# State decays of the first six attention units through DRAM on the GpSimd queue, instead of one-column matmuls and a copy

## Chip, cores and metric

One core of one Trainium2 chip runs the whole program. The metric is the device time of one execution in microseconds (us); three runs of the kernel before gave 713.31, 714.43 and 714.64 us, median 714.43.

## What is computed

Three layers follow each other. The first is an attention with a decaying state, for 4 batches and 8 heads of 48 columns over 768 positions:

```python
f = 1.0 / (1.0 + np.exp(-f_logit))
for t in range(S):
    state = f[:, :, t, :, None] * state + np.einsum('bhd,bhe->bhde', k[:, :, t], v[:, :, t])
    y[:, :, t] = np.einsum('bhd,bhde->bhe', q[:, :, t], state)
```

Its result, laid out as x of 3072 rows and 384 columns, goes through `h = x @ w_in; g = h - tanh(h); x = g @ w_out` with 2048 hidden columns. The third layer sends each row, if `x @ w_skip > 0`, to the best of 8 experts (`relu(x @ w1[e]) @ w2[e]`, weighted and added to x).

## The kernel before

The positions are cut into chunks of 128. A **unit** u is one chunk of one batch (batch u % 4), 24 in all; two units make a block of 256 rows for the second layer. Within a unit the decay is a running sum of logarithms: `pl` (PE) sums the logs of the 128 rows, `ek` and `en` (ACT) take exp of the sum and of its negative, and `mk` and `mq` (DVE) scale k and q by them. `tk`, `tq` (PE) and `ck`, `cq` (ACT) transpose both, `scores` (PE), `mask` (DVE) and `values` (PE) make the unit's output, `out1` and `out2` (ACT) copy it out, `tails` (small DMAs, by POOL for units 1 and 3 and half of unit 5, by ACT for the other half, by SP later) move 16 rows of each head pair to their place, and `xhi` (ACT) and `xlo` (DVE) split the block into a high and a low part for the products of the second layer. Only the odd unit of a block has `tails`, `xhi` and `xlo`.

Between units of one batch the state `S` must be renewed: `renew` (DVE) adds the unit's sum of k times v, and `decay` (POOL, which is GpSimd) multiplies S by the decay over the whole unit. That decay is the last row (position 127) of the tile that `en` wrote, 8 heads by 48 columns; it must come to lie down the partitions, as a tile `dd` of 112 partitions by 4, one such slice for each unit of a block. There are two ways:
- Units 0 to 5 (`u < FIRST`, FIRST is 6): at the end of `values` eight matmuls with one column each (L594) turn the row into columns of PSUM, and `renew` begins with a copy of them (L631) to `dd`.
- Units 6 to 23: `put_dec` (L505) stores the row to the DRAM tensor `dec`, and `get_dd` (L637) reads it back, for the two units of a block, by an access that puts 448 single words of 4 bytes into 112 partitions by 4. Both are issued by SP. `decay` and `in_range` (DVE, a check on the size of the decays) wait for `get_dd`.

The second layer runs in slots, one for each 128 hidden columns of a block: `G` (PE, L737, into `ph`), `T` (ACT, tanh, L743, into `th`), `bend` (DVE, L748), `ghi` (ACT, L756) and `glo` (POOL, L762), which split the result into `gs`, and `H` (PE, L779). `th` has two buffers, so `T` of slot n waits for `glo` of slot n - 2. The weights of the second layer come in 16 chunks that must be unpacked on ACT and DVE in the same stretch: `ldw` and `ld` (three indirect DMAs by POOL for a chunk pair of w_in, L367, into `stgw`; one DMA by SP for w_out), `abs`, `shift`, `stt1`, `stt2`, `hi`, `lo`.

Each engine takes its instructions strictly in the order in which they are written. That order is a list of steps, `OPENING`, written out by hand as a string up to slot 28 (in `in_order`, `listed`); the rest follows from a planner with costs. A name and a number stand for a step there: `glo.0` is `glo` of slot 0, `decay.3` is `decay` of unit 3, `ldw.4.0`, `ldw.4.1` and `ld.4` are the three loads of chunk pair 4, which is the second pair of w_in.

The tile that `en` writes (`en0`, `en1` and a part of `early`) is written again by a later unit; `read` names the step that must have read it by then. The tensor `dec` is filled with ones at the start (`preset`), so that its pad words are set.

Of the kernel before, what the change touches and what calls it, by code (L numbers as in the profile page):

```python
# [97 lines left out]
def decay_attention_moe_kernel(  # L98
# [14 lines left out]
    nc = tc.nc  # L113
# [340 lines left out]
    def attend(u):  # L454
# [4 lines left out]
        kp, qp = kpad[i], qpad[i]  # L459
        i, ze = (u, -1) if u < 3 else ((u - 3) % 2, u - 3 if u < 5 else u - 2)  # L460
        e8 = epad[i]
        read = ("values" if ze < FIRST else "put_dec", ze)
        kp8, qp8 = kp[:, :, :D], qp[:, :, :D]
        kp4 = kp.rearrange("t (p j) d -> t p (j d)", j=2)
        qp4 = qp.rearrange("t (p j) d -> t p (j d)", j=2)
# [1156 lines left out]
```

## Time and profile before

| | us |
|---|---|
| median of 3 runs (713.31 to 714.64) | 714.43 |
| the profiled execution | 713.45 |
| its span, from the first to the last instruction | 711.6 |
| PE busy | 690.3 (97%) |
| DVE busy | 494.0 (69%) |
| ACT busy | 363.7 (51%) |
| POOL busy | 294.7 (41%) |

The profiled execution's own time is 1.85 us above its span. A busy PE says little by itself, since ends of matmuls are modelled; what counts is where PE waits, for whom, and which wait ends last. A line of a timeline gives the start, the length, engine, source line, operation and tile, the number of merged instructions, and in brackets how long the engine had been idle and what ended that. "issue" is time in which an engine waited for nothing that the profile shows.

### The profile page before, as it was taken

The numbers are of one execution on the slowest core, as the hardware profiler recorded it, in microseconds if no ns is written. First come the engines' busy times: TensorE is split into PE (matmuls) and PEld (weight loads), VectorE is DVE, ScalarE is ACT, GpSimd is POOL, SyncE is SP. The second block draws the span as 40 slices with busy tenths as digits, with TensorE's granted clock in tenths as the row PEclk, the third lists the DMA queues.
The fourth block names the chain that finished last, engine by engine and source line by source line (L and its number), as shares of the span: only waits on it lengthen the run. The fifth ranks groups of instructions, "written<-read, shape, count | busy, mean of one in ns | idle before, by whom it ended". The sixth has DMA issues, their size and how long they took to land.

```text
span 711.6 us, 15497 instructions
## 1 busy us (share of the span) xinstructions
PE 690.3 (97%) x5690; PEld 623.3 (88%) x5690; DVE 494.0 (69%) x1380; ACT 363.7 (51%) x890; POOL 294.7 (41%) x340
## 2 busy tenths in 40 slices
PE   7899999999999999999999999999999999999995
PEld 4688888998888888888889888999999789999994
DVE  4889998598879576785867759469775755555531
ACT  4877665564456544464554444444444445555530
POOL 4446444224344423434335334334543314555551
PEclk9999999999999999999999999999999999999998
DMA  8995355842232132221310121024002676666500
GB/s 216 240 240 150 112 178 141 238 97 58 52 79 56 36 73 40 63 51 42 83 24 30 29 62 25 7 77 163 7 34 69 216 235 217 220 215 217 177 18 23
DMA packets 147498, 76.70 MB, mean 108 GB/s; under 512 B 113288, under 2 KB 142617, under 8 KB 147286
## 3 DMA queue, kind: packets, MB, share of 16 engines
q1 hardware_dynamic: 142550, 64.18, 33.4%
q0 software_dynamic: 4768, 11.39, 4.5%
q8 instruction: 47, 0.77, 0.4%
q14 instruction: 37, 0.30, 0.1%
q10 hardware_dynamic: 96, 0.05, 0.0%
HBM read 61.60 MB, written 15.86 MB: 109 GB/s over the span
## 4 chain that ended last, share of the span: by engine, by line
PE 79%; DVE 6%; issue 5%; POOL 3%; DMA 3%; ACT 2%; SPq 0%; POOLq 0%; ACTq 0%; DVEq 0%
PE po L779 25%; PE ph L737 24%; PE eh L1275 9%; PE eo L1299 8%; PE ps L543 3%; PE py L581 3%; POOL gs L762 2%; PE py L528 2%; DMA f<-in_f_logit_dram 1%; PE py L588 1%; PE eh L1027 1%; PE pk L512 1%; PE pq L512 1%; PE eo L1039 1%; DVE th L748 1%
## 5 line engine op out<-in xcount | busy, mean ns | idle before, releaser
L762 POOL TENSOR_TENSOR gs<-th,gs 128x256 fp32r<-128x256 f32 x190 | 161.6, 856 | 230.9 <-ACT gs L756 217.5
L779 PE MATMUL po<-uhi,gs 128*128 128x384 f32 x768 | 229.9, 347 | 2.3 <-POOL gs L762 1.9
L737 PE MATMUL ph<-xall,whi 128*128 128x256 f32 (+1 forms) x816 | 197.1, 331 | 1.4 <-DVE th L748 1.1
L737 PEld LDWEIGHTS ph<-xall,whi 128*128 128x128 f32 x816 | 138.3, 188 | 14.5 <-DVE th L748 2.2
L779 PEld LDWEIGHTS po<-uhi,gs 128*128 128x128 f32 x768 | 140.9, 188 | 9.6 <-POOL gs L762 3.9
L269 DVE CUSTOM_DVE_ANT_0 scr<-pay,wb 128x384 f32<-128x384 f32 x198 | 133.5, 674 | 8.6 <-ACT pay L788 4.4
L737 PE MATMUL ph<-xall,wlo 128*128 128x256 f32 (+1 forms) x408 | 134.0, 328 | 0.1
L779 PE MATMUL po<-ulo,gs 128*128 128x384 f32 x384 | 129.3, 337 | 0.3 <-DVE ulo L415 0.3
L756 ACT ACTIVATE gs<-th 128x256 fp32r<-128x256 f32 x192 | 79.2, 416 | 98.0 <-DVE th L748 66.3
L748 DVE TENSOR_TENSOR th<-ph,th 128x256 f32<-128x256 f32 x192 | 76.4, 417 | 71.0 <-ACT th L743 70.1
L743 ACT ACTIVATE th<-ph 128x256 f32<-128x256 f32 x192 | 68.8, 380 | 104.9 <-PE ph L737 73.1
L737 PEld LDWEIGHTS ph<-xall,wlo 128*128 128x128 f32 x408 | 77.0, 189 | 7.2 <-issue 0.3
L779 PEld LDWEIGHTS po<-ulo,gs 128*128 128x128 f32 x384 | 72.5, 189 | 2.0 <-DVE ulo L415 0.6
L1275 PE MATMUL eh<-xt,w 128*128 128x256 f32 x504 | 69.8, 283 | 0.0
L1299 PE MATMUL eo<-w,h 128*128 128x384 f32 x336 | 69.4, 342 | 0.0
L1275 PEld LDWEIGHTS eh<-xt,w 128*128 128x128 f32 x504 | 67.1, 188 | 0.4
L1299 PEld LDWEIGHTS eo<-w,h 128*128 128x128 f32 x336 | 56.5, 188 | 0.0
L1284 DVE SCALAR_TENSOR_TENSOR h<-eh,h 128x256 fp32r<-128x256 f32 x56 | 23.7, 423 | 46.1 <-ACT h L1283 46.0
L1283 ACT ACTIVATE h<-eh 128x256 fp32r<-128x256 f32 x56 | 21.6, 386 | 61.9 <-PE eh L1275 61.8
L821 POOL DMA_INDIRECT xs<-pay,dst x24 | 27.6, 1150 | 57.1 <-DVE run L829 18.8
L353 POOL TENSOR_TENSOR w<-r,w 128x768 fp32r<-128x768 f32 x24 | 44.4, 1851 | 15.0 <-ACT w L352 15.0
L999 POOL DMA_INDIRECT out_dram<-yo,xa x16 | 15.9, 994 | 63.5 <-DVE yo L1007 34.9
(198 smaller groups left out, 925.5 us busy)
## 6 DMA issues: line engine op xcount, KB each, us to landing
r<-in_moe_w_dram SPq DMA_DIRECT2D x56, 384.0 KB
stgu<-in_moe_w_out_dram SPq DMA_DIRECT2D x4, 1536.0 KB
f<-in_f_logit_dram SPq DMA_DIRECT2D x24, 192.0 KB
out_dram<-pay SPq DMA_DIRECT2D x24, 192.0 KB
k<-in_k_dram SPq DMA_DIRECT2D x22, 192.0 KB
q<-in_q_dram SPq DMA_DIRECT2D x22, 192.0 KB
v<-in_v_dram SPq DMA_DIRECT2D x22, 192.0 KB
xs<-zrow SPq DMA_DIRECT2D x2, 1544.0 KB
```

Of the source, the lines that this page charges most:

```text
L269: nc.vector.tensor_tensor_reduce(out=scr, in0=x, in1=wb[:, n], scale=1.0, scalar=0.0, op0=ALU.mult, op1=ALU.add, accum_out=lg[:, n : n + 1])
L353: eng.tensor_tensor(lo, raw, hi.bitcast(F32), ALU.subtract)
L737: nc.tensor.matmul(ph, lhsT=w[:, i, fs], rhs=x[:, i, a], start=(n == 0), stop=(n == 3 * KT - 1))
L743: nc.scalar.activation(th, ph, AF.Tanh)
L748: nc.vector.tensor_tensor(th, ph, th, ALU.subtract)
L756: nc.scalar.activation(t[:, 0], th, AF.Copy)
L762: eng.tensor_tensor(t[:, 1], th, t[:, 0].bitcast(F32), ALU.subtract)
L779: nc.tensor.matmul(po[blk, s], lhsT=t[:, a, ss], rhs=w[:, f], start=(f == first_f[blk] and n == 0), stop=(f == last_f[blk] and n == 2),)
L821: nc.gpsimd.indirect_dma_start(xs[:, :], bass.IndirectOffsetOnAxis(ap=di, axis=0), pt[:, :], None, bounds_check=E * NT - 1, oob_is_err=False,)
L1275: nc.tensor.matmul(ph, lhsT=a1[:, w, i, f * P : (f + 1) * P], rhs=xt[:, i, a], start=(n == 0), stop=(n == 3 * KT - 1))
L1284: nc.vector.scalar_tensor_tensor(out=h[:, 1], in0=ph, scalar=0.0, in1=h[:, 0].bitcast(F32), op0=ALU.max, op1=ALU.subtract)
L1299: nc.tensor.matmul(eo[e, s], lhsT=h[:, a, ss], rhs=a2[:, w, f], start=(f == 0 and n == 0), stop=(f == NF2 - 1 and n == 2))
```

## The change

Units 0 to 5 now also take the way through DRAM, by POOL's own DMA queue. The 48 one-column matmuls and the 6 copies are gone. `put_dec` and `get_dd` of these units are instructions of POOL; `decay` of both units of a block comes after `get_dd` and after each one's `renew`; `in_range` waits for `get_dd`; and the tile that `en` wrote is free once `put_dec` has read it. OPENING is written anew, with the new steps at their places. On PE, ACT and SP the instructions that both kernels have stand in the same order; on DVE `in_range` of unit 3 moves and the copies go; on POOL the decays move and the new DMAs come in. Behind OPENING nothing moves.

```diff
     LAG = 2
     TAILS_BY = ["PP", "PP", "AP"]
     OPENING = (
...
-        "ln.2 k.2 mq.1 f.3 abs.0 pl.2 renew.0 f.4 decay.0 tq.1 out1.0 shift.0 out2.0 ld.2 cq.1 stt1.0 ek.2 k.3 scores.1 en.2 stt2.0 "
...
+        "ck.1 q.2 min.2 values.0 ln.2 get_dd.1 k.2 mq.1 f.3 abs.0 pl.2 renew.0 f.4 tq.1 out1.0 shift.0 out2.0 ld.2 cq.1 stt1.0 ek.2 "
...
@@
-        read = ("values" if ze < FIRST else "put_dec", ze)
+        read = ("put_dec", ze)
...
+        how = nc.gpsimd if u < FIRST else nc.sync
+
         def put_dec():
-            nc.sync.dma_start(dec[u : u + 1, :].rearrange("u (h d) -> u h d", h=H)[:, :, :D], e8[P - 1 : P, :, :D])
+            how.dma_start(dec[u : u + 1, :].rearrange("u (h d) -> u h d", h=H)[:, :, :D], e8[P - 1 : P, :, :D])
...
@@ in values
-            if u < FIRST:
-                for h in range(H):
-                    p, j = divmod(h, 2)
-                    nc.tensor.matmul(
-                        pu[64 * j : 64 * j + 64, 2 * P + p : 2 * P + p + 1], lhsT=e8[:, h], rhs=ident[:, P - 1 :],
-                        start=True, stop=True,
-                    )
...
@@ in renew
-            if u < FIRST:
-                if half == 0:
-                    dds[blk] = apool.tile([112, 2, NP], F32, tag="dd", name=f"dd{u}", bufs=2)
-                nc.vector.tensor_copy(dds[blk][:, half], m["pu"][:112, 2 * P : 2 * P + NP])
...
@@ in get_dd
             for i in range(2):
-                nc.sync.dma_start(dds[blk][:, i], dec[u - 1 + i].rearrange("(p a) -> a p", a=P)[:112])
+                how.dma_start(dds[blk][:, i], dec[u - 1 + i].rearrange("(p a) -> a p", a=P)[:112])
...
@@ in the list of steps
-        if u >= FIRST:
-            step(("put_dec", u), at(1), "SP", 0.6, put_dec, ("en", u), ("preset", 0), moved=0.1)
+        if True:
+            step(("put_dec", u), at(1), "SP" if u >= FIRST else "POOL", 0.6, put_dec, ("en", u), ("preset", 0), moved=0.1)
...
-            *(old if u < FIRST and half == 0 else []), give=(("pa", f"u{u}" if u < FIRST else f"y1_{u}"),),
-        )
-        if u < FIRST:
-            step(("decay", u), at(4), "POOL", 0.7, decay(u), ("renew", u))
+            give=(("pa", f"u{u}" if u < FIRST else f"y1_{u}"),),
+        )
         if half:
-            if u >= FIRST:
-                step(("get_dd", u), at(3.5), "SP", 1.0, get_dd, ("put_dec", u), ("put_dec", u - 1), *old, moved=0.2)
+            if True:
+                step(("get_dd", u), at(3.5), "SP" if u >= FIRST else "POOL", 1.0, get_dd, ("put_dec", u), ("put_dec", u - 1), *old, moved=0.2)
                 for w in (u - 1, u):
                     step(("decay", w), at(4), "POOL", 0.82, decay(w), ("get_dd", u), ("renew", w))
-            step(("in_range", u), at(5), "DVE", 0.16, in_range, *([("get_dd", u)] if u >= FIRST else [("renew", u - 1), ("renew", u)]))
+            step(("in_range", u), at(5), "DVE", 0.16, in_range, ("get_dd", u))
```

What that does to the order. **POOL, from the second load of w_in (`stgw1`) to slot 3.** `dec<-en` is `put_dec`, `dd<-dec` is `get_dd`, `S<-S,dd` is `decay`, `gs<-th,gs` is `glo`, `xf<-tm` is `tails`. Before:

```order
L622 DMA early_81<-early_81 16x256 x6
L367 DMA stgw1_493<-in_moe_w_in_dram,rowid_71 128x1024 x3
L642 TENSOR_TENSOR S2_110<-S2_110,dd2_584 112x4x48
L762 TENSOR_TENSOR gs0_0_643<-th0_0_614,gs0_0_643 128x256
L762 TENSOR_TENSOR gs0_1_686<-th0_1_647,gs0_1_686 128x256
L762 TENSOR_TENSOR gs0_2_688<-th0_2_676,gs0_2_688 128x256
L622 DMA xf2_580<-tm2_581 16x256 x6
L642 TENSOR_TENSOR S3_111<-S3_111,dd2_584 112x4x48
L762 TENSOR_TENSOR gs0_3_787<-th0_3_740,gs0_3_787 128x256
```

The same place on POOL with the change:

```order
L618 DMA early_81<-early_81 16x256 x6
L368 DMA stgw1_480<-in_moe_w_in_dram,rowid_71 128x1024 x3
L508 DMA dec_64<-en1_117 8x1x48
L508 DMA dec_64<-en0_116 8x1x48
L629 DMA dd3_547<-dec_64 112x4x1 x2
L752 TENSOR_TENSOR gs0_0_624<-th0_0_595,gs0_0_624 128x256
L752 TENSOR_TENSOR gs0_1_659<-th0_1_628,gs0_1_659 128x256
L634 TENSOR_TENSOR S2_110<-S2_110,dd3_547 112x4x48
L634 TENSOR_TENSOR S3_111<-S3_111,dd3_547 112x4x48
L752 TENSOR_TENSOR gs0_2_661<-th0_2_649,gs0_2_661 128x256
L618 DMA xf2_564<-tm2_565 16x256 x6
L508 DMA dec_64<-en0_116 8x1x48
```

`put_dec` of units 4 and 3 and both DMAs of `get_dd.3` now stand between the loads of `stgw1` and `glo.0`; `decay.2` has moved behind `glo.1`, and `decay.3` from behind `tails` of unit 3 to before `glo.2`.

**DVE, from slot 2 to the low part of w_out.** `qp` is `mq`, `S<-pu` is `renew`, `okd` is `in_range`, `ulo` is `lo`. Before:

```order
L748 TENSOR_TENSOR th0_2_676<-ph0_2_633,th0_2_676 128x256
L502 TENSOR_TENSOR qp0_114<-q4_486,en1_117 128x8x48
L631 COPY dd2_584<-pu3_659 112x4
L632 TENSOR_TENSOR S3_111<-pu3_659,S3_111 112x4x48
L415 SCALAR_TENSOR_TENSOR ulo_693<-dcu0_483,uhi_84 128x768
L415 SCALAR_TENSOR_TENSOR ulo_693<-dcu1_514,uhi_84 128x768
L499 TENSOR_TENSOR kp1_113<-k5_435,kp1_113 128x8x48
L647 SCALAR_TENSOR_TENSOR okd_77<-dd2_584,okd_77 112x8
```

The same place on DVE with the change:

```order
L738 TENSOR_TENSOR th0_2_649<-ph0_2_614,th0_2_649 128x256
L503 TENSOR_TENSOR qp0_114<-q4_473,en1_117 128x8x48
L624 TENSOR_TENSOR S3_111<-pu3_640,S3_111 112x4x48
L639 SCALAR_TENSOR_TENSOR okd_77<-dd3_547,okd_77 112x8
L416 SCALAR_TENSOR_TENSOR ulo_666<-dcu0_470,uhi_84 128x768
L416 SCALAR_TENSOR_TENSOR ulo_666<-dcu1_501,uhi_84 128x768
L500 TENSOR_TENSOR kp1_113<-k5_424,kp1_113 128x8x48
```

The copy is gone, and `in_range` of unit 3 (`okd`) stands ahead of the two `lo` steps instead of behind them and `mk`; it now reads what `get_dd.3` brings.

## Rows read from the trace of the kernel before

**Rows 1.** The page: busy us by engine, and PE's busy tenths in 40 slices.

```profile
PE 690.3 (97%) x5690; PEld 623.3 (88%) x5690; DVE 494.0 (69%) x1380; ACT 363.7 (51%) x890; POOL 294.7 (41%) x340
PE   7899999999999999999999999999999999999995
```

**Rows 2.** Windows: length, then busy us of each engine, clock, DMA share, GB/s.

```profile
40.00:50.00 10.00, 10.00 (x142) 9.02 (x141) 9.85 (x18) 7.15 (x20) 6.44 (x10) 1.00 0.80 222
80.00:90.00 10.00, 10.00 (x71) 9.45 (x70) 9.97 (x15) 6.94 (x16) 5.29 (x5) 1.00 0.14 33
```

**Rows 3.** The chain that ended last, from 45 to 54 us: start, us, what.

```profile
45.34 1.00 POOL xf L622 x2
...
47.85 4.53 DMA xf<-tm
...
52.59 0.84 ACT xall L653
```

**Rows 4.** PE's timeline at the one-column matmuls of units 2 and 4.

```profile
35.07 0.60 PE L594 MATMUL pu<-ident,early 128*64 128x1 f32 x16
35.59 0.76 PE L737 MATMUL ph<-xall,whi 128*128 128x256 f32 x2
...
53.25 0.60 PE L594 MATMUL pu<-ident,en 128*64 128x1 f32 x16
53.78 0.38 PE L737 MATMUL ph<-xall,whi 128*128 128x256 f32 x1
54.47 0.39 PE L737 MATMUL ph<-xall,whi 128*128 128x256 f32 x1 [0.31 <-DVE xall L657]
```

**Rows 5.** DVE's timeline: the copy of unit 4, and what follows.

```profile
55.14 0.15 DVE L631 COPY dd<-pu 112x4 f32<-112x4 f32 x1
55.21 0.35 DVE L632 TENSOR_TENSOR S<-pu,S 112x192 f32<-112x192 f32 x1
```

**Rows 6.** POOL's timeline: decays, loads of w_in, glo and tails.

```profile
26.23 1.16 POOL L642 TENSOR_TENSOR S<-S,dd 112x192 f32<-112x192 f32 x1 [6.66 <-DVE S L632]
...
33.49 0.99 POOL L367 DMA_INDIRECT stgw<-in_moe_w_in_dram,rowid  x1 [0.30 <-issue]
...
40.44 0.74 POOL L762 TENSOR_TENSOR gs<-th,gs 128x256 fp32r<-128x256 f32 x1 [3.06 <-ACT gs L756]
43.25 2.14 POOL L762 TENSOR_TENSOR gs<-th,gs 128x256 fp32r<-128x256 f32 x2 [2.07 <-ACT gs L756]
...
48.45 0.52 POOL L642 TENSOR_TENSOR S<-S,dd 112x192 f32<-112x192 f32 x1
50.30 1.28 POOL L762 TENSOR_TENSOR gs<-th,gs 128x256 fp32r<-128x256 f32 x1 [1.33 <-ACT gs L756]
```

**Rows 7.** By tile (xf to 50 us; stgw, dec, whole run): ns min/median/max of one.

```profile
L622 POOL DMA_DIRECT2D xf<-tm x6: 484/506/582, 45.3 to 47.9; - x6
L367 POOL DMA_INDIRECT stgw<-in_moe_w_in_dram,rowid x12: 993/1111/1661, 5.8 to 91.0; - x12
DMA to landing us min/median/max: 4.8/6.1/7.1
L637 SPq DMA_DIRECT2D dd<-dec x18: 320/462/1637, 105.8 to 457.3; - x18
```

**Rows 8.** ACT's timeline at slots 1 and 2.

```profile
41.43 0.39 ACT L743 ACTIVATE th<-ph 128x256 f32<-128x256 f32 x1 [0.75 <-PE ph L737]
42.03 0.84 ACT L411 ACTIVATE uhi<-dcu 128x768 fp32r<-128x768 f32 x1 [0.21 <-DVE dcu L234]
42.78 0.71 ACT L756 ACTIVATE gs<-th 128x256 fp32r<-128x256 f32 x2
```

**Rows 9.** Windows of POOL alone: length, POOL busy, clock, DMA share, GB/s.

```profile
38.00:40.00 2.00, 0.00 (x0) 1.00 1.09 290
40.00:41.00 1.00, 0.56 (x1) 1.00 0.36 66
```

**Rows 10.** Timelines: ACT's xall of unit 5, PE's first H after slot 2, PE's last long wait.

```profile
69.97 0.85 ACT L653 ACTIVATE xall<-xf 128x768 fp32r<-128x768 f32 x1 [0.87 <-DMA xf<-tm]
...
57.17 0.44 PE L779 MATMUL po<-uhi,gs 128*128 128x384 f32 x1
...
73.99 0.50 PE L737 MATMUL ph<-xall,whi 128*128 128x256 f32 x2 [0.93 <-DVE th L748]
```

More of the change, by code (lines that the diff above doesn't have):

```diff
@@ L697, in attend @@
             ("renew", u), at(3.5), "DVE", 0.5 if u < FIRST else 0.36, renew, ("values", u), ("out1", u) if u >= FIRST else None,
-            *(old if u < FIRST and half == 0 else []), give=(("pa", f"u{u}" if u < FIRST else f"y1_{u}"),),
+            give=(("pa", f"u{u}" if u < FIRST else f"y1_{u}"),),
         )
-        if u < FIRST:
-            step(("decay", u), at(4), "POOL", 0.7, decay(u), ("renew", u))
         if half:
-            if u >= FIRST:
-                step(("get_dd", u), at(3.5), "SP", 1.0, get_dd, ("put_dec", u), ("put_dec", u - 1), *old, moved=0.2)
+            if True:
+                step(("get_dd", u), at(3.5), "SP" if u >= FIRST else "POOL", 1.0, get_dd, ("put_dec", u), ("put_dec", u - 1), *old, moved=0.2)
                 for w in (u - 1, u):
                     step(("decay", w), at(4), "POOL", 0.82, decay(w), ("get_dd", u), ("renew", w))
-            step(("in_range", u), at(5), "DVE", 0.16, in_range, *([("get_dd", u)] if u >= FIRST else [("renew", u - 1), ("renew", u)]))
+            step(("in_range", u), at(5), "DVE", 0.16, in_range, ("get_dd", u))
             for j in range(2):
                 if u >= FIRST:
-                    how = "SP", 1.4, tails(j, nc.sync)
+                    by = "SP", 1.4, tails(j, nc.sync)
                 else:
-                    how = {"A": ("ACT", 1.9, tails(j, nc.scalar)), "P": ("POOL", 1.7, tails(j, nc.gpsimd)), "S": ("SP", 1.9, tails(j, nc.sync))}[TAILS_BY[blk][j]]
-                step(("tails", u, j), at(3.5), *how, ("out2", u), moved=0.1)
+                    by = {"A": ("ACT", 1.9, tails(j, nc.scalar)), "P": ("POOL", 1.7, tails(j, nc.gpsimd)), "S": ("SP", 1.9, tails(j, nc.sync))}[TAILS_BY[blk][j]]
+                step(("tails", u, j), at(3.5), *by, ("out2", u), moved=0.1)
             step(("xhi", u), at(4), "ACT", 0.84, xhi, ("tails", u, 0), ("tails", u, 1), ("lastG", blk - AHEAD - 1))
```

49 rows, old and new, of the table OPENING are left out of this document.

## Prediction

> **What bounds the kernel now.** The page first: PE is busy 97% of the span, and of its 40 slices only the first two and the last lie below nine tenths [rows 1]. PE's last wait of some length ends at 73.99 us [rows 10], and from 80 to 90 us it has no gap at all [rows 2]: what the change brings must come from the first 74 us, and what it delays there stays, since little idle time is left behind to take it up. Next the windows: from 40 to 50 us PE shows 10.00 and DVE 9.85 of 10 us [rows 2], so busy time doesn't tell which of them sets the pace. The chain of waits does: at 45.34 us it runs through POOL's six small DMAs (`tails` of unit 3), their landing 4.53 us after the last issue at 47.85, that is 52.38, and ACT's `xhi` at 52.59 [rows 3]; then through DVE's `xlo`, for which PE's G waits 0.31 us at 54.47 [rows 4]. So here POOL, nowhere the busiest engine [rows 1], is on the path, and what stands ahead of `tails` on POOL counts in full.
>
> **What the change removes.** On PE 48 one-column matmuls. Sixteen records make one unit's eight; they begin at 35.07 and the next product at 35.59, so a unit costs 0.52 us, six 3.1 us [rows 4]. I credit none of it. For unit 2 the product behind needs `xlo` of unit 1: its first two records stretch over 0.76 us, where one alone takes 0.38, so it would start earlier only to wait there. For unit 4 the product at 53.78 waits for DVE at 54.47 [rows 4]. For unit 3 the work behind is ahead of `tails`' landing and PE arrives early anyway. Units 0 and 1 lie where PE waits for ACT and DVE. On DVE six copies: begun at 55.14, with the next at 55.21, one costs 0.07 us [rows 5]. Two of them lie behind 52.59 on DVE's part of the path: 0.15 us gained.
>
> **What it adds, and the prices.** On POOL six stores and six reads (three pairs). A store has 8 pieces; the nearest row is a POOL DMA of 16 rows at 0.51 us [rows 7]: I take 0.5. A read is 448 separate words, and no row shows POOL issuing one. By count the nearest are 16 rows at 0.506 and the indirect loads of 128 rows at 0.993 us at least (that one, since a direct DMA reads no list of offsets) [rows 7]: 4.35 ns a row, so 0.506 + 432 x 0.00435 = 2.4 us. That is my price of one read. The lower end is 0.5, if the count costs nothing. The upper end is 3.9, if it grows in proportion from 128 rows at 1.11. SP's price for the same access, a median of 0.46 us [rows 7], speaks for the lower end, but another engine issues it. [...]
>
> **The first pair is hidden.** `put_dec` of units 0 and 1 and `get_dd.1` stand where POOL does nothing for long: it waits 6.66 us even for the decay at 26.23, which needs DVE's `renew` [rows 6]. The loads of `stgw0` land at most 7.1 us after issue [rows 7]; two reads at 2.4 behind that leave room before 26.2. Should a read cost 3.9, `const` behind it on POOL is late, and DVE waits for what it writes.
>
> **The second pair is not.** With the change POOL has, behind the third load of `stgw1`, which ends at 33.49 + 0.99 = 34.5 [rows 6], both stores (to 35.5), the read of unit 2, and the read of unit 3, which waits for unit 3's store to land; behind that wait stand `glo.0`, `glo.1`, the decays, `glo.2` and `tails`. When does the store land? 4.5 us after its issue at 35.0, by the small DMA of [rows 3], is 39.5; the loads ahead of it on the same queue keep the DMA engines full (1.09) to 40 us, and the next window shows 0.36 [rows 9]. I take 40.0. Then:
> - the read is issued from 40.0 to 42.4, and `glo.0` runs to 43.15; before, it ended at 40.44 + 0.74 = 41.18 [rows 6];
> - T of slot 2 waits for `glo.0`: 43.2 for 41.43, 1.8 us late. Behind it ACT had waited 0.21 for DVE, which is now over, so `ghi.1` is 1.6 late [rows 8];
> - `glo.1` begins at 43.25 + 1.6 = 44.85. From there to `tails` it was 45.34 - 43.25 = 2.09 us; now both decays lie between, at 0.5 each (0.52 [rows 6]): 47.95, for 45.34, **2.6 us late**. `decay.3` also needs its data; 4.5 us after the issue at 40.0 they are there, ahead of it;
> - `tails` had 52.59 - 52.38 = 0.2 us to spare [rows 3]: `xhi` is 2.4 late, and with it `xlo`, G and the rest of the path.
>
> **The third pair and the last decays are hidden**, just so. `put_dec.5` and `get_dd.5` hold up `glo.3`, which ended at 50.30 + 1.28 [rows 6], until about 58.5 (`tails` over at 51.0, store 51.5, first read 53.9, landing about 56, second read 58.4, then `glo.3`); the H that needs it came at 57.17 [rows 10] and would now come 2.4 later, at 59.6. `decay.4`, now ahead of `tails` of unit 5, adds 0.5 there, but ACT's `xhi` waits 0.87 us for the half of `tails` on ACT's queue [rows 10].
>
> **The sum**: +2.4 - 0.15 = +2.25 us on the profiled execution, 713.45 + 2.25 = 715.7. The median of the runs shown is 714.43, 0.98 above that execution, so I forecast **716.7 us**. With a read between 1.7 and 3 us it is 716 to 717.5.
>
> **Rivals.** A change of 0.2%, 1.4 us, is about what a measurement of this kernel can tell from none.
> - *Reads are cheap* (0.5 us). `glo.0` ends at 41.25, as good as on time; only the two decays, 1.0 us, are new ahead of `tails`: 1.1 late, less 0.2 and 0.15, +0.75, so 715.2. [...]
> - *Faster: PE sets the pace.* If from 35 to 62 us it is PE, without a gap from 40 to 50 [rows 2], and not POOL's `tails` that decides, the one-column matmuls of units 2 to 4, 3 x 0.52, and the copies are gained: -1.7, so 712.7. It decides only if the store of unit 3 lands before 39.5 and a read costs 0.5, so that POOL still reaches `tails` by 45.5; against it speaks the chain, which has POOL and DMA there.
> - *Heavier*: a read at 3.9 us puts `glo.0` at 44.65, 3.5 late, `tails` 4.1 late; and where the data land only 4.5 us behind the end of such an issue, at 48.4, `decay.3` waits a further 1.4 us, and `in_range.3`, now ahead of two `lo` steps, holds up DVE. +3.8 to +5.3, so 718.2 to 719.7.
> - *The words really travel in another way than I count* (a read lowered to 112 pieces) is the first rival with a price between, some 1.0 us, and falls to its upper edge.
>
> **Chances**: forecast 0.51, cheap reads 0.24, PE sets the pace 0.11, heavier 0.14. The forecast's lower edge touches 1.4 us, so slower by over 0.2% has 0.63, within 0.2% 0.26, faster 0.11. The range runs from 713.7 (cheap reads, less the scatter of the runs shown) to 719.7; it leaves out the faster case and a part of the heavier one.
>
> **What would show it.** Right: no L594 and no L631; POOL idle before `get_dd.3`'s second DMA until about 40 us, put down to the store's landing; that DMA at about 2.4 us; ACT's T of slot 2 waiting for POOL about 1.8 us; `tails` of unit 3 beginning near 48; the same gap of PE before G, some 2.4 us later; after 80 us all of it shifted evenly. Wrong: a read at 0.5 us, `tails` at 46 or earlier, or PE reaching 74 us' work sooner than before. A fall of PE's clock at another place than before would spoil the comparison of a stretch and is in none of these sums.

## The result, and the profile after

The changed kernel takes **723.91 us** (median of 4 runs, 720.48 to 725.06), the kernel before 714.53 beside it (4 runs, 713.31 to 715.40): a ratio of 1.0122, interval 1.0101 to 1.0142. That is 9.4 us more where 2.25 were forecast. Timed again in a later comparison (e16 below) it was 1.0068 (1.0046 to 1.0090): always slower, but by an amount that varies. The profiled execution took 725.06 us, with a span of 723.3 (before 711.6).

The page, against [rows 1]: POOL has 9.7 us more of busy time and PE 5.4, though PE lost 96 of its matmul records.

```profile
PE 695.7 (96%) x5594; PEld 626.7 (87%) x5594; DVE 493.3 (68%) x1374; ACT 364.0 (50%) x890; POOL 304.4 (42%) x352
PE   7897999999999999999999999999999999999994
```

Windows after, against [rows 2] (length, busy us of PE, PEld, DVE, ACT, POOL, then granted clock, DMA share, GB/s):

```profile
40.00:50.00 10.00, 10.00 (x85) 8.53 (x78) 7.52 (x14) 5.83 (x15) 5.11 (x4) 0.69 0.54 171
50.00:60.00 10.00, 6.84 (x105) 6.03 (x103) 4.53 (x9) 4.05 (x10) 7.00 (x12) 0.99 1.05 187
60.00:70.00 10.00, 9.12 (x71) 8.27 (x72) 7.18 (x12) 7.01 (x14) 5.09 (x5) 0.50 0.21 62
80.00:90.00 10.00, 9.07 (x62) 8.47 (x61) 10.00 (x15) 6.32 (x15) 3.76 (x4) 1.00 0.57 177
```

PE now idles for 3.2 of the 10 us from 50 to 60, and from 60 to 70 its granted clock is 0.50, called half the clock below. Before, both windows showed a clock of 1.00:

```profile
50.00:60.00 10.00, 9.24 (x137) 8.02 (x136) 8.27 (x15) 8.48 (x17) 3.45 (x3) 1.00 0.73 133
60.00:70.00 10.00, 9.54 (x99) 9.00 (x95) 8.39 (x14) 6.56 (x19) 8.81 (x10) 1.00 0.58 188
```

POOL's timeline after, against [rows 6]. Lines have shifted: L508 is `put_dec`, L629 `get_dd`, L752 `glo`, L634 `decay`, L618 `tails`.

```profile
35.87 1.11 POOL L508 DMA_DIRECT2D dec<-en  x2
36.96 0.76 POOL L629 DMA_DIRECT2D dd<-dec  x1
42.46 0.73 POOL L629 DMA_DIRECT2D dd<-dec  x1 [4.74 <-DMA dec<-en]
43.20 1.48 POOL L752 TENSOR_TENSOR gs<-th,gs 128x256 fp32r<-128x256 f32 x1
47.10 0.73 POOL L752 TENSOR_TENSOR gs<-th,gs 128x256 fp32r<-128x256 f32 x1 [2.41 <-ACT gs L746]
47.78 3.57 POOL L634 TENSOR_TENSOR S<-S,dd 112x192 f32<-112x192 f32 x2
51.31 1.04 POOL L752 TENSOR_TENSOR gs<-th,gs 128x256 fp32r<-128x256 f32 x1
52.30 3.21 POOL L618 DMA_DIRECT2D xf<-tm  x6
```

The second read waits 4.74 us for the store and takes 0.73; the two `decay` products take 3.57 together; `tails` begins at 52.30 for 45.34. By line, the two DMAs that [rows 7] could only bound (ns min/median/max of one):

```profile
L629 POOL DMA_DIRECT2D dd<-dec x6: 720/742/759, 16.0 to 59.8; - x6
```

```profile
L508 POOL DMA_DIRECT2D dec<-en x5: 518/545/598, 9.8 to 55.5; - x5
```

The narrow view of the first product, and DVE at that moment (the copy of [rows 5] is gone ahead of L624):

```profile
47.78 3.11 POOL L634 TENSOR_TENSOR S<-S,dd 112x192 f32<-112x192 f32 x1
```

```profile
47.37 0.36 DVE L624 TENSOR_TENSOR S<-pu,S 112x192 f32<-112x192 f32 x1 [0.46 <-PE pu L591]
47.64 0.21 DVE L639 SCALAR_TENSOR_TENSOR okd<-dd,okd 112x8 f32<-112x8 f32 x1
47.77 1.81 DVE L416 SCALAR_TENSOR_TENSOR ulo<-dcu,uhi 128x768 fp32r<-128x768 f32 x2
49.51 0.55 DVE L500 TENSOR_TENSOR kp<-k,kp 128x384 f32<-128x384 f32 x1
49.98 0.54 DVE L503 TENSOR_TENSOR qp<-q,en 128x384 f32<-128x384 f32 x1
```

`decay.2` lasts 3.11 us, six times the 0.52 of [rows 6], and ends at 50.89, 0.37 us behind DVE's row `ulo`, `ulo`, `kp`, `qp`, which ends at 50.52. So it lasts about as long as four DVE steps in a row (2.75 us from 47.77), and not as long as one. All four take both inputs from SBUF; no run varies that. *Held*, below, is only a name for a POOL step that lasts 3.0 to 3.5 us beside this row; by what means DVE would hold it isn't shown.

ACT at slots 1 and 2, against [rows 8]; both T wait for PE, which ran at a clock of 0.69 there, and not for POOL:

```profile
43.62 0.38 ACT L733 ACTIVATE th<-ph 128x256 f32<-128x256 f32 x1 [1.83 <-PE ph L727]
45.60 0.38 ACT L733 ACTIVATE th<-ph 128x256 f32<-128x256 f32 x1 [1.60 <-PE ph L727]
```

The chain and what hangs on it, against [rows 3], [rows 4] and [rows 10] (the chain, then ACT, then PE):

```profile
55.03 4.28 DMA xf<-tm
```

```profile
59.54 0.84 ACT L645 ACTIVATE xall<-xf 128x768 fp32r<-128x768 f32 x1 [5.02 <-DMA xf<-tm]
```

```profile
60.44 0.58 PE L727 MATMUL ph<-xall,whi 128*128 128x256 f32 x1 [3.59 <-ACT xall L645]
...
83.95 0.50 PE L727 MATMUL ph<-xall,whi 128*128 128x256 f32 x2 [0.93 <-DVE th L738]
```

`xhi` is 6.95 us late, PE stands 3.59 us for it and goes on at half the clock (0.50 from 60 to 70 us), and PE's last long wait ends at 83.95, 9.96 late. The tanh of slot 20, before and after, is 10.64 late:

```profile
99.76 0.36 ACT L743 ACTIVATE th<-ph 128x256 f32<-128x256 f32 x1
```

```profile
110.40 0.37 ACT L733 ACTIVATE th<-ph 128x256 f32<-128x256 f32 x1
```

From there to the end of the second layer all is shifted evenly (10.65 at the last tanh). What lies behind the last tanh, the third layer for the most part, adds 1.0; its length scatters by 2.6 us over the profiles. Of the shift some 1.3 us is there from the beginning (`tails` of unit 1 at 28.62 for 27.34); over all profiles, with and without the change, that start lies between 26.8 and 29.9.

### The profile page after: what moved, and what is told of

Same layout as the page of the kernel before. It is cut to its first block, busy times and chain, and to the rows that moved or that the text cites. A ratio compares the mean times of both kernels' runs of the same rounds, so it can differ in the third digit from the quotient of the medians.

```text
span 723.3 us, 15316 instructions
## 1 busy us (share of the span) xinstructions
PE 695.7 (96%) x5594; PEld 626.7 (87%) x5594; DVE 493.3 (68%) x1374; ACT 364.0 (50%) x890; POOL 304.4 (42%) x352
## 3 DMA queue, kind: packets, MB, share of 16 engines
q0 software_dynamic: 5152, 11.41, 4.6%
## 4 chain that ended last, share of the span: by engine, by line
PE 80%; DVE 6%; issue 5%; POOL 4%; DMA 3%; ACT 1%; POOLq 0%; ACTq 0%; DVEq 0%
PE po L769 25%; PE ph L727 24%; PE eh L1265 8%; PE eo L1289 8%; PE ps L546 3%; PE py L584 3%; POOL gs L752 2%; PE py L531 2%; PE pk L515 1%; PE py L591 1%; DMA xs<-pay,dst 1%; PE pq L515 1%; PE eo L1029 1%; DMA dec<-en 1%; DVE th L738 1%
## 5 line engine op out<-in xcount | busy, mean ns | idle before, releaser
L752 POOL TENSOR_TENSOR gs<-th,gs 128x256 fp32r<-128x256 f32 x190 | 162.0, 857 | 229.4 <-ACT gs L746 215.9
L727 PE MATMUL ph<-xall,whi 128*128 128x256 f32 (+1 forms) x816 | 200.5, 335 | 6.9 <-ACT xall L645 4.7
L727 PEld LDWEIGHTS ph<-xall,whi 128*128 128x128 f32 x816 | 141.1, 192 | 20.5 <-ACT xall L645 5.0
L727 PEld LDWEIGHTS ph<-xall,wlo 128*128 128x128 f32 x408 | 78.6, 193 | 6.9
```

What stands on the lines that cost most here:

```text
L727: nc.tensor.matmul(ph, lhsT=w[:, i, fs], rhs=x[:, i, a], start=(n == 0), stop=(n == 3 * KT - 1))
L752: eng.tensor_tensor(t[:, 1], th, t[:, 0].bitcast(F32), ALU.subtract)
```

## The experiments

All ratios are against runs of the kernel before on the same chip (medians there 713.87 us for e1 to e4, 715.74 for e5 to e12, 714.76 for e13 to e16, 714.27 for e17 and e18), taken over all runs and so not exactly the quotient of two medians. Profiles are of one execution each.

**Which part of the order costs: e1, e2.** Both move steps of the second pair behind `tails` of unit 3; e2 also moves the third pair's reads behind `glo.3`.

```diff
 e1
-renew.3 decay.2 decay.3 in_range.3 out1.3
+renew.3 in_range.3 out1.3
-tails.3.0 put_dec.5
+tails.3.0 decay.2 decay.3 put_dec.5
```

> The changed kernel with the decays of units 2 and 3 behind the tails of unit 3 on GpSimd; the wait of the second read pair stays. Theory (GpSimd is on the path at these tails, and the decay of unit 2 was held there for 3.11 us beside VectorE's low-part steps): tails of unit 3 begin about 3.5 us earlier than the 52.30 us of the changed kernel, and the time falls by 3 us or more, to about 719 to 721. Rival (only TensorE's clock and the landing of the store make the loss): no change, 722 to 725.

Measured 717.47 us, 1.0055 (1.0036 to 1.0074): the theory held, with more gained than it asked. `tails` begins at 46.09. But `in_range.3`, which the change put ahead of `ulo` on DVE, waits 3.13 us for the read's landing, and PE's H of slot 0 then 2.59 for `ulo`.

```diff
 e2
-exp.5 get_dd.3 put.0
+exp.5 put.0
-renew.3 decay.2 decay.3 in_range.3 out1.3
+renew.3 out1.3
-tails.3.0 put_dec.5
+tails.3.0 put_dec.5 get_dd.3
-get_dd.5 mask.4.0 exp.7 glo.3
+mask.4.0 exp.7 glo.3 get_dd.5 decay.2 decay.3
-renew.4
+renew.4 in_range.3
```

> The changed kernel with the second read pair, its decays and its range check behind the tails of unit 3, the third read pair behind the glo of slot 3; all else as in the changed kernel. Theory (the order on GpSimd ahead of the tails is the whole loss, the clock follows it): tails of unit 3 begin by 47 us, the clock stays up from 50 to 74 us, and the time is 713 to 717, no slower than before. Rival (less work on TensorE lets its clock fall by itself): still 719 or more, with half-clock stretches of more than 10 us in the first 75 us.

Measured 721.05, 1.0100 (1.0072 to 1.0129): the theory missed. Of the new steps only two stores (1.09 us) still stood ahead of `tails`, and yet `glo.1`, 0.73 us elsewhere, took 3.46 us beside the same row of DVE, `tails` came at 49.34, and the clock was halved from 57.8 to 68.0 us (a line of two 128x256 products of PE lasts 0.63 us there, for 0.40 at 41.62). So it isn't only the `decay` that is slow there: `glo` is too.

**Is it the missing PE work: e3, e4.** e3 puts the 48 matmuls back and leaves their result unused; e4 adds 56 matmuls of 128x128 after `values` of unit 4.

```diff
 e3, in values
+            if u < FIRST:
+                for h in range(H):
+                    p, j = divmod(h, 2)
+                    nc.tensor.matmul(
...
+                    )
```

> The changed kernel with the 48 one-column matmuls put back, their result not used. Theory (GpSimd's waits): tails of unit 3 begin as late as in the changed kernel, about 52 us, and the time is 723 to 727. Rival (the clock falls because the one-column matmuls are gone): the clock is as before the change, with one half-clock stretch near 30 us, and the time goes back to 718 or less.

```diff
 e4, in values
+            if u == 4:
+                for _ in range(56):
+                    nc.tensor.matmul(pu[:, 3 * P :], lhsT=ones, rhs=ones, start=True, stop=True)
```

> The changed kernel with 56 small matmuls of no use behind the values of unit 4, where TensorE waited 3.6 us for the tails of unit 3. Theory (the wait for the tails lets the clock fall from 60 to 70 us, which costs some 3 us more): the clock stays at its upper level from 60 to 70 us, the tails begin as in the changed kernel, and the time is 720 to 721.5. Rival (the stretch at the lower clock costs nothing, since other engines set the pace there): 723 to 725.

e3 721.88, 1.0117 (1.0098 to 1.0136): putting the matmuls back doesn't cure the changed kernel; `decay.2` was held 3.13 us as before. e4 723.78, 1.0136 (1.0111 to 1.0160): the clock stayed up behind `xhi` (a line of two 128x256 products lasts 0.40 us from 65 to 72 us, for 0.63 at 62 in the change), but `renew` of unit 4 waited 2.78 us for the added matmuls, and in its profile the loss comes earlier than the gap that was filled (`in_range.3` waits 3.25 us, PE 3.39 for `ulo`), so it prices nothing.

**The parts alone, in the kernel before: e5, e6.** e6 also takes the block `if u < FIRST` with the matmuls out of `values`, as the change does.

```diff
 e5
-out2.2 decay.2 ln.5
+out2.2 ln.5
-renew.3 out1.3
+renew.3 decay.2 decay.3 out1.3
-q.6 decay.3 mask.4.0
+q.6 mask.4.0
 e6, in renew
-                nc.vector.tensor_copy(dds[blk][:, half], m["pu"][:112, 2 * P : 2 * P + NP])
+                nc.vector.tensor_copy(dds[blk][:, half], m["pu"][:112, :NP])
```

> The kernel before, nothing through DRAM, with one thing of the change alone: on gpsimd the state products of units 2 and 3 stand where the change has them, both directly behind renew.3 and so ahead of glo.2 and of tails.3.0 (before, decay.2 stood behind glo.0's predecessor and decay.3 behind tails.3.0). Theory (a gpsimd product that falls beside DVE's back-to-back steps with two SBUF inputs is held for the length of those steps, 3.1 us instead of 0.5): tails.3 starts 1 to 3.5 us later than the 45.34 us of before, one of the products or glo.2 lasts over 1.5 us, and the time is 715.5 to 718. Rival (the long product came only from the later, waited-for read, and the placing alone costs its 0.5 us at most): every product lasts 0.5 to 0.8 us, the time is within 1 us of before.

Measured 716.36, 1.0005 (0.9987 to 1.0023): the rival's time; the placing cost nothing that can be told. The profile lies between: the products took 1.22 and 0.50 us and `glo.2` 1.45, while DVE's two `ulo` took 2.66 together, for the 1.81 of the change. POOL reached the place 0.53 us ahead of `ulo` here, so this run didn't try the meeting of the change.

> The kernel before without the 48 products with one column of units 0 to 5; the copy on DVE stays and reads other columns of the same PSUM tile, so the state decays are other numbers: it leaves out the sum that gives the decays. The prediction credited PE's 3.1 us with nothing, its rival with 1.7 us. By the prediction: 713.5 to 714.9, no difference that can be told. By the rival: 712 to 713. If a removal of PE's work lets the granted clock fall where it did not before: up to 717, with a new stretch at half the clock.

The wrong decays sent the program down its slow path for decays out of range, 7401 us: nothing is learnt from the time. e13 repeats it.

**What e1 left over: e7, e8.**

```diff
 e7: e1 and
-renew.3 in_range.3 out1.3
+renew.3 out1.3
-renew.4
+renew.4 in_range.3
 e8: e7 and
-tk.3 ldw.4.0
+tk.3 put_dec.3 put_dec.4 ldw.4.0
-ld.4 put_dec.4 put_dec.3 tk.4
+ld.4 tk.4
```

> The change with the products of units 2 and 3 behind tails.3.0 (as in the first run of the series) and, new, in_range.3 on DVE moved from ahead of lo.2 and lo.3 to behind renew.4. Theory (in_range.3 held DVE 3.1 us for the landing of the second read, ulo came late, H.0 on PE waited 2.6 us for it): that wait is gone, H.0 starts 2 us or more earlier, and the time is 715 to 717 against 717.5. Rival (H.0's wait is covered by the later tails, xhi still ends last): within 0.7 us of 717.5.

> As the run before it, and the stores of units 3 and 4 stand on gpsimd ahead of the three loads of the first expert's second weights instead of behind them. Theory (the store's landing is late because it stands behind 1.5 MB of loads on one queue): it lands in about 3 us, the read is issued without the 5 us wait, glo.0 starts at once on its own inputs, tails.3 goes out within 1 us of the 45.3 us of before, and the time is 713.5 to 716. Rival (the landing takes 5 us wherever it stands, or the loads that now start 1.1 us later are on the path): no better than the run before it.

Both theories missed: e7 719.97, 1.0055 (1.0040 to 1.0070), no better than e1; e8 722.30, 1.0075 (1.0057 to 1.0092). In e8 POOL waits for no landing of the second pair, and still `tails` starts at 49.73. POOL and DVE of e8 show why:

```profile
45.69 3.40 POOL L753 TENSOR_TENSOR gs<-th,gs 128x256 fp32r<-128x256 f32 x1 [2.07 <-ACT gs L747]
```

```profile
45.75 1.81 DVE L417 SCALAR_TENSOR_TENSOR ulo<-dcu,uhi 128x768 fp32r<-128x768 f32 x2
```

The wait of `in_range.3` in e1 had kept `ulo` away from `glo.1` (48.08 and 44.73 us); with that wait gone, the two begin level (45.20 and 45.21 in e7).

**Taking `tails` out of reach: e9 to e12.** e9 is e7 with `mk.5` and `mq.5` behind `bend.3`, so that DVE's row has two steps. e10 puts `tails` first, e11 adds e8's early stores to it, e12 does e10's move of `tails` in the kernel before.

```diff
 e9: e7 and
-H.0 mk.5 f.9 T.3 mq.5 tails.3.0
+H.0 f.9 T.3 tails.3.0
-bend.3 shift.4
+bend.3 mk.5 mq.5 shift.4
 e10
-glo.1 ulo.0 renew.3 decay.2 decay.3 in_range.3 out1.3 lo.2 out2.3 tq.4 glo.2
+ulo.0 renew.3 out1.3 lo.2 out2.3 tails.3.1 tails.3.0 glo.1 decay.2 decay.3 tq.4 glo.2
-lo.3 tails.3.1 cq.4
+lo.3 cq.4
-mq.5 tails.3.0 put_dec.5
+mq.5 put_dec.5
-renew.4
+renew.4 in_range.3
 e11: e10 and e8's move of put_dec.3 and put_dec.4
 e12, in the kernel before
-glo.1 ulo.0 renew.3 out1.3 lo.2 out2.3 tq.4
+ulo.0 renew.3 out1.3 lo.2 out2.3 tails.3.1 tails.3.0 glo.1 tq.4
-lo.3 tails.3.1 cq.4
+lo.3 cq.4
-mq.5 tails.3.0 scores.4
+mq.5 scores.4
```

> The kernel of the run with in_range.3 late (e7), and on DVE the two products kp and qp of unit 5 stand behind bend.3 instead of directly behind the two ulo steps. Theory (gpsimd's step is held for the whole unbroken row of DVE steps with two inputs in SBUF, not for one of them): glo.1, which took 3.34 us there beside four such steps of 3.0 us together, takes 1.8 to 2.4 us beside the two that are left, and tails.3 starts about 1 us earlier against the same start. Rival (gpsimd's step is slow by itself, or waits for one step only): glo.1 keeps 3.3 us or falls to 1.4 or less. The time may go either way, since kp of unit 5 comes later; 717 to 721.

Measured 717.54, 1.0027 (1.0007 to 1.0047). `glo.1` wasn't held at all, it began 0.62 us ahead of `ulo`; `glo.2` took 1.49 beside the two `ulo`, which took 2.37 together. So the question of the row's length wasn't tested. The time is below e7's, with intervals that overlap; whether the shorter row or the lead gained it isn't shown.

> The change with tails.3 on gpsimd directly behind glo.0, ahead of glo.1, glo.2 and the products of units 2 and 3, and in_range.3 behind renew.4. The wait for the store's landing stays ahead of it, the held steps come behind it. Theory (what costs is what stands ahead of tails.3): tails.3 starts at 43 to 45 us instead of 52.3, xhi of the second pair at 50 to 53 instead of 59.5, the clock does not fall at 58 to 70 us, and the time is 714.5 to 718. Rival (the loss is mainly the clock and the late glo steps, or glo.1 now late holds PE): 719 or more.

> As the run before it, with the stores of units 3 and 4 ahead of the three loads as in e8, so that gpsimd waits for no landing. Theory: glo.0 at 41 to 42 us, tails.3 at 43 to 44 us, and the time 713.5 to 716.5, level with the kernel before. Rival: nothing more than in the run before it, since T.0 and out2 set tails.3 then; 714.5 to 718.

> The kernel before, with tails.3 directly behind glo.0 and ahead of glo.1 and glo.2 on gpsimd; nothing else changed. If tails.3 and what follows it sets the pace there too: tails.3 starts at 43.2 us instead of 45.3, xhi of the second pair 2 us earlier, and the time is 711.5 to 713.5, the best of all. If the later glo.1 and glo.2 then hold PE's H steps: no gain, or up to 2 us lost.

e10 718.10, 1.0038 (1.0022 to 1.0055); e11 716.12, **1.0004** (0.9987 to 1.0020), level with before; e12 715.77, 1.0006 (0.9986 to 1.0025), no gain. In their profiles `tails` began at 45.20, 45.78 and 45.02 us, after 2.2 to 2.8 us of waiting for ACT's `tm`, where 43 to 45 was expected; e10's time lies just above its range. POOL in e11:

```profile
42.29 0.73 POOL L753 TENSOR_TENSOR gs<-th,gs 128x256 fp32r<-128x256 f32 x1 [2.94 <-ACT gs L747]
45.78 2.93 POOL L619 DMA_DIRECT2D xf<-tm  x6 [2.76 <-ACT tm L607]
48.72 0.75 POOL L753 TENSOR_TENSOR gs<-th,gs 128x256 fp32r<-128x256 f32 x1
```

Its six `tails` ran beside the same DVE row (`ulo` from 45.20) at 0.49 to 0.53 us each: issuing a DMA wasn't held there, as POOL products were. From the change to e11 every new instruction is still there; only places differ. The landing wait ahead of `glo.0` is worth e10 less e11, 2.0 us by the medians (their intervals all but touch).

**The open terms: e13 to e16.** e13 is e6 with another copy, e14 the change with the stores and reads on SP's queue (the planner's engine of both steps changes with it), e15 is e11 with the edit of e14, e16 the change again.

```diff
 e13, in renew
+                nc.vector.tensor_copy(dds[blk][:, half], tri[:112, P - 1 :].bitcast(F32).to_broadcast([112, NP]))
 e14
-        how = nc.gpsimd if u < FIRST else nc.sync
+        how = nc.sync
```

> The kernel before without the 48 products with one column of units 0 to 5; the copy on DVE reads a column of ones in SBUF in place of the sums, so every state decay of the first three pairs is 1.0: it leaves out the computation of these decays. By the prediction (PE's 3.1 us are worth nothing by themselves): level with before, ratio 0.998 to 1.002. By the rival that PE sets the pace: 0.996 to 0.998. If the missing products let the granted clock fall at 40 to 46 us as in e6: 1.001 to 1.004, with that stretch in the profile.

> The change with the stores and reads of units 0 to 5 issued on sync's queue instead of gpsimd's, at the same places of the order; the products of units 2 and 3 stay ahead of glo.2 and tails.3. Theory (the order ahead of tails.3 and DVE's row cost most, the landing wait some 2 us, as e11 against e10): glo.0 at 41 to 42 us, but in_range.3 or one of gpsimd's steps still late, tails.3 at 47 to 50, ratio 1.003 to 1.009. Rival (gpsimd's queue is the whole cause): tails.3 at 45 to 46.5 and a ratio of 1.002 or less.

> As e11 (tails.3 behind glo.0, stores of units 3 and 4 ahead of the loads, in_range.3 late), with the stores and reads on sync's queue, so that gpsimd has neither. Theory: the first stage is bound by PE then, as in the kernel before: level with e11 and with before, ratio 0.998 to 1.002. If freeing gpsimd of 7 us of issues is worth something: under 0.998, a version that beats both. If sync's loads wait behind a store for its exponential: over 1.002.

> The changed kernel once more, unaltered, beside the others. Expected: a ratio of 1.009 to 1.014 as before. If the stretch at half the clock at 58 to 70 us follows from PE's wait for the second pair's xhi, it is there again, and the second state product or a glo step ahead of tails.3 lasts 3 us again; if it was chance, it is not there and the time is 3 us shorter.

e13 718.34, **1.0045** (1.0023 to 1.0067): taking PE's work away, with no DMA added, makes the kernel slower. That the third layer gets other numbers with these decays doesn't explain it: what lies behind the last tanh takes 164.3 us in e13's profile and 164.4 in that of before. POOL, DVE and PE of e13:

```profile
43.48 3.01 POOL L755 TENSOR_TENSOR gs<-th,gs 128x256 fp32r<-128x256 f32 x1 [2.08 <-ACT gs L749]
```

```profile
43.60 1.81 DVE L415 SCALAR_TENSOR_TENSOR ulo<-dcu,uhi 128x768 fp32r<-128x768 f32 x2
```

```profile
55.37 0.38 PE L730 MATMUL ph<-xall,whi 128*128 128x256 f32 x1 [2.59 <-ACT xall L646]
```

`glo.1` is held again. e14 719.45, 1.0060 (1.0035 to 1.0085): without any of the new DMAs on POOL, as slow as the change here; POOL's queue by itself isn't the cause. (Its profile is of its second fastest execution, 716.34 us, and can't show that loss.) e15 717.02, 1.0023 (1.0002 to 1.0044): no version that beats both. e16 720.51, 1.0068 (1.0046 to 1.0090), below what was expected. Its profile shows the loss by another way, POOL and DVE:

```profile
45.52 0.51 POOL L634 TENSOR_TENSOR S<-S,dd 112x192 f32<-112x192 f32 x1
48.07 0.51 POOL L634 TENSOR_TENSOR S<-S,dd 112x192 f32<-112x192 f32 x1 [2.04 <-DMA dd<-dec]
```

```profile
48.02 0.17 DVE L639 SCALAR_TENSOR_TENSOR okd<-dd,okd 112x8 f32<-112x8 f32 x1 [3.12 <-DMA dd<-dec]
```

Here POOL arrived so early that the read hadn't landed: `decay.3` waits 2.04 us and `in_range.3` 3.12. On DVE `in_range.3` keeps `ulo` waiting, and so PE. DVE, PE, ACT and the window of e16 behind that:

```profile
48.16 2.77 DVE L416 SCALAR_TENSOR_TENSOR ulo<-dcu,uhi 128x768 fp32r<-128x768 f32 x2
```

```profile
50.12 0.69 PE L769 MATMUL po<-ulo,gs 128*128 128x384 f32 x1 [3.27 <-DVE ulo L416]
```

```profile
57.96 0.60 ACT L522 ACTIVATE kT<-pk 112x512 f32<-112x512 f32 x1 [4.55 <-PE pk L515]
58.46 0.83 ACT L645 ACTIVATE xall<-xf 128x768 fp32r<-128x768 f32 x1
```

```profile
50.00:60.00 10.00, 9.88 (x75) 8.79 (x75) 7.26 (x12) 5.05 (x11) 5.32 (x9) 0.54 0.60 113
```

PE stands 3.27 us for `ulo` and works on at half the clock (48.9 to 59.2 us); ACT's `ck` waits 4.55 for PE, and `xhi` follows it at 58.46 without a wait of its own. So in this profile `xhi` is 5.9 us late by way of `in_range.3`, DVE and PE, and not by `tails`, which began 3.85 late at 49.19. e1 and e4 show the same wait of PE. These two profiles of the change show one loss each: POOL's product held beside DVE's row, or DVE held by `in_range.3`; they differ in when slots 1 and 2 came.

**What decides whether POOL is held: e17, e18.** The POOL product that came first at the two `ulo` steps, by its lead over them (e1, e10 to e12 and e15 have no product there at that moment):

| profile | POOL step begins | first `ulo` begins | lead, us | step lasts, us |
|---|---|---|---|---|
| e9, `glo.1` | 46.01 | 46.63 | 0.62 | 0.72 |
| e5, `glo.1` | 44.11 | 44.64 | 0.53 | 0.73 |
| e18, `glo.1` | 43.00 | 43.52 | 0.52 | 0.72 |
| before, `glo.1` | 43.25 | 43.62 | 0.37 | 0.72 |
| e13, `glo.1` | 43.48 | 43.60 | 0.12 | 3.01 |
| e2, `glo.1` | 45.24 | 45.36 | 0.12 | 3.46 |
| e17, `glo.1` | 45.13 | 45.24 | 0.11 | 3.00 |
| e8, `glo.1` | 45.69 | 45.75 | 0.06 | 3.40 |
| e7, `glo.1` | 45.21 | 45.20 | -0.01 | 3.33 |
| e3, `decay.2` | 48.12 | 48.13 | 0.01 | 3.13 |
| after, `decay.2` | 47.78 | 47.77 | -0.01 | 3.11 |
| e4, `decay.3` | 49.51 | 49.61 | 0.10 | 0.51 |
| e16, `decay.3` | 48.07 | 48.16 | 0.09 | 0.51 |
| e14, `decay.3` | 46.24 | 45.93 | -0.31 | 1.01 |

For `glo.1` the lead tells the two cases apart: short from 0.37 us on, held at 0.12 or less. For the `decay` products it doesn't: `decay.3`, which had waited for the read just before, wasn't held at a lead of 0.10 and 0.09, and in e14, 0.31 behind `ulo`, it lasted 1.01 us, twice its 0.50 and not the length of the row. What else decides is open. By the recorded starts POOL came first in five of the held cases, by 0.01 to 0.12 us, so coming first by so little isn't enough.


Of `glo.1`, e17 takes the lead from the kernel before, e18 gives it to e13.

```diff
 e17, ghi, in the kernel before
+        if (blk, f) == (0, 1):
+            nc.scalar.activation(t[:, 1], th, AF.Copy)
         nc.scalar.activation(t[:, 0], th, AF.Copy)
 e18, at the end of renew, in e13
+            if u == 3:
+                nc.vector.tensor_copy(m["pu"][:112, 2 * P : 2 * P + NP * D], m["pu"][:112, : NP * D])
```

> The kernel before with one more ACT copy of 128x256 (0.35 us) directly ahead of ghi.1, into the half of the tile that glo.1 overwrites, so that glo.1 on gpsimd starts some 0.35 us later against DVE's first ulo step and the lead of 0.37 us is gone. Theory (the order in which the two engines come decides): glo.1 lasts 3.0 to 3.5 us instead of 0.73, tails.3 starts 2 us or more later, the time grows by 2 to 4 us (ratio 1.002 to 1.006). Rival (the lead is no cause): glo.1 lasts 1.5 us at most and the ratio is 0.999 to 1.0015, the copy's own 0.35 us at most.

> The kernel of e13 (the 48 products out, decays of 1.0: it leaves out the computation of these decays) with one more DVE copy of 112x192 inside PSUM (about 0.3 us) between renew.3 and the first ulo step, so that glo.1 has its lead again. Theory: glo.1 lasts 0.73 to 1.5 us instead of 3.01, tails.3 is back at 45 to 46 us against the same start, and the ratio falls from 1.0045 to 0.999 to 1.002. Rival (the loss of e13 is the products' missing and the clock, not the step on gpsimd): the ratio stays at 1.003 to 1.006.

POOL and DVE of e17, then of e18:

```profile
45.13 3.00 POOL L764 TENSOR_TENSOR gs<-th,gs 128x256 fp32r<-128x256 f32 x1 [2.38 <-DVE dd L631]
45.24 1.81 DVE L415 SCALAR_TENSOR_TENSOR ulo<-dcu,uhi 128x768 fp32r<-128x768 f32 x2
```

```profile
43.00 2.14 POOL L757 TENSOR_TENSOR gs<-th,gs 128x256 fp32r<-128x256 f32 x2 [2.07 <-ACT gs L751]
43.25 0.37 DVE L627 COPY pu<-pu 112x192 f32<-112x192 f32 x1
43.52 2.44 DVE L415 SCALAR_TENSOR_TENSOR ulo<-dcu,uhi 128x768 fp32r<-128x768 f32 x2
```

Both profiles went as the theory says. In time e18 did too: 714.86, 1.0009 (0.9992 to 1.0026), for e13's 1.0045 in the comparison before: **adding** 0.37 us of DVE work ahead of the row won back what taking PE's work away had lost (two comparisons, whose intervals overlap by 0.0003). e17 did not: 715.34, 1.0013 (0.9994 to 1.0032), the rival's range. Its profiled execution took 718.0, 2.7 above its median, so most of its 12 runs may have kept the lead; that isn't shown.

**The clock.** It was never varied by itself. Over the profiles, e6 left aside: in the seven in which PE idled for 2.6 to 3.6 us in one piece that ended between 49 and 61 us (after, e1, e2, e4, e8, e13, e16) the granted clock fell to 0.5 between 1.2 us before and 0.6 us behind that end, and stayed there for 3.4 to 10.2 us. In the twelve others, with no idle piece above 1.5 ending there, only e3, e15 and e17 show a stretch that begins there. In after, e2 and e8 that stretch lies behind `xhi` for 10.2 us, and the tanh of slot 20 follows `xhi` by 50.7 to 51.0 us; without any stretch behind `xhi` (before, e1, e5, e7, e9 to e12, e14, e16, whose stretch ends with `xhi`, and e18) by 46.9 to 49.2. The difference, 1.5 to 4.1 us, is what the clock may add to such a wait: a comparison of kernels that differ in other things too, not an experiment. From 60 to 70 us, e8 and e18:

```profile
60.00:70.00 10.00, 10.00 (x105) 9.18 (x105) 6.75 (x14) 6.53 (x13) 3.41 (x4) 0.60 0.40 116
```

```profile
60.00:70.00 10.00, 8.72 (x72) 7.77 (x69) 8.19 (x14) 5.98 (x16) 9.00 (x10) 1.00 0.61 188
```

## Why the prediction was right on the sign and wrong on the size

- **Place: right in part.** POOL ahead of `tails` of unit 3 was on the path in the first profile, and the first pair stayed hidden. In e16's profile the path ran through `in_range.3` on DVE, which the sum put at nothing and only the heavier rival named. e11, with the same instructions in another order, is level with before; it moves both.
- **"That is my price of one read", 2.4 us: too high.** It is 0.74 us, six reads between 0.720 and 0.759 in the first profile, between the first rival's 0.5 and the last one's 1.0. That each of the 448 words adds to it was the author's estimate and no run shows it; the six stores and six reads together added 384 packets on queue q0 (4768 on the page before, 5152 after).
- **"I take 40.0" for the store's landing: too early.** POOL waited to 42.46, or to 41.82 in e16, which has no late start (`tails` of unit 1 at 27.23). The two errors cancel: 2.4 + 40.0 gave 42.4 for the start of `glo.0`, and e16 has 42.57. A sum that meets its number at one point isn't thereby right in its terms.
- **"`glo.1` begins at 44.85": 47.10.** Of the 2.25 some 1.3 is the late start; for the rest T of slots 1 and 2 waited for PE, at a clock of 0.69 from 40 to 50 us, and not for POOL. In e16 T of slot 2 did wait for POOL (2.67 us), and `glo.1` began at 44.83, as forecast.
- **"Both decays lie between, at 0.5 each", and the data "are there, ahead of it": the step that failed.** From `glo.1` to `tails` the sum has 3.1 us; the first profile has 5.20, since the decays took 3.11 and 0.50, and e16 has 4.36, since 2.04 of waiting stood between its two decays of 0.51. The duration came from a row of POOL beside other DVE work; the place it moved to, beside DVE's `ulo`, `ulo`, `mk`, `mq`, was never looked at. The landing was taken at 4.5 us behind the read's issue; the step that needed it started 6.2 us behind that issue in e16 (41.82 to 48.02). The same late landing held `in_range.3`, and with it DVE 3.12 us and PE 3.27.
- **The shift behind `xhi`: not even.** The sum carries the delay of `xhi` unchanged to the end. In the first profile it grows from 6.95 at `xhi` to 10.64 at the tanh of slot 20, over the stretch at half the clock; how much of the 3.7 us is the clock's wasn't separated. **The clock "is in none of these sums"**: it should have been a rival of its own, since its own sum has PE standing 2.4 us longer before G.
- **"I credit none of it", PE's 3.1 us: a loss, not nothing.** e13 put it at +0.45% (0.23 to 0.67), 3.2 us of 714.76 lost. e18 speaks for a changed meeting of POOL and DVE, and not for the lost work itself. e13's copy also reads SBUF instead of PSUM; that part wasn't tried apart.

The shift of the first profile, 11.7 us of span for 2.25 forecast, adds up so: 2.6 at `tails` as forecast, 1.3 of late start, 1.0 of late T, 2.1 of held products, 3.7 behind `xhi`, 1.0 behind the last tanh. That is one execution's account; the first comparison's 9.4 us and e16's 5.75 have other shares. So the range, 713.7 to 719.7, missed by 4.2 us; in e16 by 0.8.

## What to carry to other kernels

A step's duration holds for its neighbours (a decay product: 0.52 us before, 3.11 in the change's first profile). Before moving a GpSimd product, look at what DVE does at its new place, and don't let it begin level with a row of DVE steps like `ulo`, `ulo`, `mk`, `mq` (`glo.1` was held at a lead of 0.12 us or less, and took 0.72 to 0.73 at 0.37 or more), or issue what the path needs ahead of it (e11, 1.0004). Taking work from one engine shifts who comes first elsewhere (e13, 1.0045), so price a removal by the meetings it changes as well as by its length. A step whose result nobody needs soon, like `in_range`, still holds its engine when it waits for a landing ahead of work that others need (in e16 DVE 3.12 us, and PE 3.27 behind it). And a new wait of PE may cost more than its length: each of the seven long ones seen here, 2.6 to 3.6 us, came with a fall of the clock to 0.5.

## What the runs showed of the hardware

- A GpSimd product of 0.5 to 0.73 us lasted 3.0 to 3.5 us where it began level with DVE's row `ulo`, `ulo`, `mk` and on, or up to 0.12 us ahead of it (after, e2, e3, e7, e8, e13, e17), and 0.72 to 0.73 with a lead of 0.37 or more (before, e5, e9, e18); one added step turned it, a copy of 0.37 us on DVE in e18, a copy of 128x256 on ACT in e17 (one of that size takes 0.40 in the kernel before, `ghi` at 39.96). Two exceptions, `decay.3` in e4 and e16, took 0.51 at a lead of 0.10 and 0.09, and there DVE's two `ulo` took 2.78 and 2.77 together, for 1.81 beside a held step. With the lead, both engines took longer: `glo.1` and `glo.2` 2.14 together in the kernel before, for 1.42 in e1, where no `ulo` ran beside them, and the two `ulo` 2.60, for the same 1.81.
- GpSimd's issue of six small DMAs beside the same DVE row took 2.93 us, 0.49 to 0.53 each (e11; e10 also 2.93), for 3.10 in the kernel before.
- GpSimd issued a read of 448 single words in 0.74 us and a store of 8 pieces in 0.55 (medians of six and five in the change's first profile). Behind three loads on the same queue POOL waited 4.5 to 6.1 us for the store's landing (after, e1, e3, e4, e7, e10, e16); for the third pair, with no loads just ahead, 1.65 to 3.0 us (after, e1, e3, e4, e7, e8).
